# A gated linear recurrence and a squared-ReLU layer on one core: transfers of the first gates over three queues, the activation table loaded first, identity and mask made later, and a new order of the first 640 entries of the schedule

## The chip, the core and the metric

The kernel runs on one core of one Trainium2 chip. The core has five instruction queues that run side by side: TensorE (PE, matrix products; PEld is its weight load), VectorE (DVE), ScalarE (ACT), GpSimd (POOL) and SyncE (SP). Transfers between the device's memory and the core's on-chip memory are issued by SP, ACT or POOL and carried out by 16 DMA engines. The metric is the device time of one execution in microseconds (us); lower is better.

## The reference

Two blocks follow each other. The first keeps, for each of 4 x 8 heads, a complex 48 x 48 state that is multiplied at each of 768 steps by a complex gate (with its magnitude held below 0.999), takes in the product of key and value, and is read out by the query. The second is a two-layer network with a squared ReLU on the 3072 x 384 result.

```python
mag = np.sqrt(a_re * a_re + a_im * a_im)
scale = np.minimum(mag, 0.999) / (mag + 1e-06)
a_re_n, a_im_n = (a_re * scale, a_im * scale)
for t in range(S):
    new_re = ar * S_re - ai * S_im
    new_im = ar * S_im + ai * S_re
    kv = np.einsum('bhd,bhe->bhde', k[:, :, t], v[:, :, t])
    S_re, S_im = (new_re + kv, new_im)
    y[:, :, t] = np.einsum('bhd,bhde->bhe', q[:, :, t], S_re)
...
h = np.maximum(x @ w_in, 0.0)          # x: 3072 x 384, w_in: 384 x 2048
return (h * h @ w_out)                  # w_out: 2048 x 384
```

The inputs q, k, v, a_re and a_im are float32; the two weight matrices arrive as float64 and are turned into float32 on the chip.

## The kernel before

Each sequence of 768 tokens is cut into 6 chunks of 128 tokens. Two chunks of two sequences (b = 0 and b = 1) make a group, and there are 12 groups (gi = 0 to 11). A group goes through three stages. First its operands are made by DVE and ACT: the gates are normalised, their running products inside a chunk are built in blocks of eight steps, and queries and keys are multiplied with them. Then each chunk is worked by PE: products of keys and queries, a causal mask on DVE, products with the values, and the new state. Last, the two layers are applied to the group's 256 tokens: for each part of the hidden layer a product with w_in (lines 1052 and 1068), a squared ReLU on ACT, and products with w_out (line 1088 for the first two groups, line 1158 later, where seven half products with sums of halves stand in for eight).

Nothing here is ordered by a compiler. The string FRONT is a list of some 1,380 entries, written out by hand, and `follow` calls the function of each entry in turn. Every engine therefore works through its instructions in the order of the list, and waits on semaphores only for what another engine or a transfer has to deliver. An entry is a letter with numbers. Those that matter here:

- `l0.0.0` and `l0.0.1` load the gates (a_re and a_im) of group 0 for b = 0 and b = 1; `l0.1.0` and `i0.1.0` load its queries and keys, the upper heads by SP and the lower by POOL. Each load is one transfer of 48 rows ("whole") and two or more of 16 rows ("gap"), in lines 527 and 532.
- `f0` fetches the first block of weight words by SP and `j0` the rest of the same block by POOL in two transfers (line 695); `f2`, `j2` and so on do it for other blocks. Three blocks are held at a time.
- `p0.k` and `q0.k` are the steps of making group 0's operands for b = 0 and b = 1. On ACT: p0.0 squares (L776), p0.1 and p0.2 the parts in the blocks' order (L761), p0.4 inverse root (L795), p0.5 (L799), p0.8 and p0.9 (L761), p0.10 (L822), p0.12 negated imaginary parts (L836), p0.14 keys (L853, L761). On DVE: p0.3 (L790), p0.7 (L494, L808), p0.11 the gates (L828, L494, L832), p0.13 (L848), p0.15 the first step in blocks (L494), p0.17 and p0.19 totals and carries, p0.20 and p0.28 to p0.30 the products. p0.21 sends the last heads by SP (L904).
- `U0` and `S0` take the low and high part of weight block 0 on ACT (L621, L628); `D0` and `A0` decode it on DVE (L635 and a custom instruction). The parts are kept in two places, so U4 overwrites what A2 reads.
- `a0.0` to `a0.9` are the work on group 0's first chunk: a0.0 scores on PE (L948), a0.1 and a0.3 transposes on PE with the identity (L956), a0.5 the product with the mask on DVE, a0.6 values on PE (L975), a0.7 the copy of the tokens on ACT (L986), a0.8 what is added to the state (L999, with two small instructions on POOL, L1005). `b0.k` is the second chunk.
- `g0.0` moves rows of x to their places with two transfers by SP (L1044), after which `F0.1.0` is the first long product on PE (L1052) and `H0.1.0` its squared ReLU.
- `M0` to `M8` are small preparations. M0 is an activation whose only use is that its table is loaded; M1 turns the causal mask on ACT and PE (lines 572 to 577); M2 to M8 set tiles to zero on DVE.

Before the list starts, POOL makes the identity and a plain triangular mask (lines 547 to 556), and DVE sets a few constants.

Of the kernel before, what the change touches and what calls it, by code (L numbers as in the profile page):

```python
# [27 lines left out]
ALU = mybir.AluOpType  # L28
# [398 lines left out]
def quotient_path(ctx, tc, feat, vtok, w_in, w_out, w1, w2, out, n_seq, count):  # L427

    nc = tc.nc
# [75 lines left out]
    def load_parts(gi, part=None, second=False, only=None):  # L505
# [7 lines left out]
        for b, n in enumerate(groups[gi]):  # L513
            if only not in (None, b):
                continue
            for hh, queue in enumerate(queues):
                if queue is None:
                    continue
                gap = raw[pads(hh), parts, b]
                rest = feat[n, hh].rearrange("(r g) x p t -> r x g p t", g=NG)[:, parts, :, NG]  # L520
                pieces = [(slice(None), i) if gap.shape[1] < NG else (slice(None), slice(None), i)
                          for i in range(min(gap.shape[1:3]))]
                moves = [(gap[at], rest[at]) for at in pieces]
                whole = (raw[rows(hh), parts, b].rearrange("d x g t -> d x (g t)"),
                         feat[n, hh, :, parts, 0:NG].rearrange("d x g t -> d x (g t)"))
                if part == 0 and b:
                    queue.dma_start(out=whole[0], in_=whole[1])
                    queue = nc.gpsimd
                else:
                    moves.insert(len(moves) if part == 0 else 0, whole)  # L530
                for to, of in moves:
                    queue.dma_start(out=to, in_=of)

    def in_turn(rows_, n):

# [3 lines left out]
    def load_values(gi, only=None):  # L539
        for b, n in enumerate(groups[gi]):  # L540
            if only not in (None, b):
# [15 lines left out]

    def turn_mask(step):
        if step == 0:

            nc.scalar.activation(out=sums[:, 0:1], in_=tiny, func=AF.Abs_reciprocal_sqrt)
            return
        if step > 1:

# [579 lines left out]
    def half_product(i, z):  # L1144
        if z == 0:
            o_of[i, 0] = po.tile([P, DM], F32, tag="o", name="o_ps")
        if z == 1:
            o_of[i, 1] = ph.tile([P, 2, TOK], F32, tag="h", name="o_ps").rearrange(
                "p j t -> p (j t)")
        lower = range(KH // 2)  # L1150
# [11 lines left out]
    def outputs(i, r):  # L1162
# [2 lines left out]
                out_of[i, b] = ffn.tile([P, DM], F32, name="o")  # L1165
        o, left, right = [out_of[i, b] for b in range(GC)], slice(0, MH), slice(MH, DM)
        chain = o_of[i, 0][:, 0:MH]
        others = [o_of[i, 1][:, k * MH:(k + 1) * MH] for k in range(2)] if r else None
        if r == 0:
            twice(o[0][:, left], chain)  # L1170
        elif r == 1:
# [18 lines left out]


    FRONT = (
        "l0.0.0 l0.0.1 M1 M0 p0.0 p0.1 p0.3 p0.4 p0.5 p0.7 M2 M3 p0.2 q0.0 q0.3 M8 M6 M7 p0.9 "
        "p0.8 q0.4 p0.10 q0.5 p0.11 l0.1.0 f0 f1 f2 i0.1.0 j0 j2 q0.1 p0.12 q0.7 p0.15 D0 p0.23 "
        "p0.24 p0.25 U0 q0.10 p0.6 p0.22 q0.8 p0.13 S0 q0.9 q0.2 p0.14 p0.16 A0 U2 p0.26 M5 j1 "
        "i0.1.1 U1 S1 S2 D2 p0.27 q0.11 p0.17 j3 i1.2.0 j4 q0.12 p0.18 D1 q0.15 p0.19 l0.1.1 "
        "q0.22 f3 l1.2.0 v0.0 f5 q0.23 p0.28 q0.24 M4 p0.20 q0.25 p0.29 q0.16 p0.30 q0.26 q0.13 "
        "q0.27 p0.21 f4 a0.1 a0.0 A1 q0.17 a0.5 A2 q0.14 q0.6 p1.6 a0.2 U3 a0.3 a0.4 q0.18 S3 "
        "a0.6 l1.2.1 q0.19 U4 a0.7 S4 D3 D4 A3 i1.2.1 j5 j6 j7 a0.8 p1.0 q0.28 p1.3 q0.20 q1.0 "
        "D5 q0.29 q1.3 q0.30 U5 p1.4 p1.5 g0.0 f6 F0.1.0 S5 q0.21 p1.7 A4 a0.9 b0.1 p1.2 p1.10 "  # L1200
        "p1.8 p1.9 p1.1 U6 b0.2 p1.11 A5 b0.0 f7 v0.1 p1.12 H0.1.0 S6 U7 p1.22 p1.15 b0.5 p1.23 "
        "D6 p1.24 D7 f8 F0.0.0 b0.6 b0.3 b0.7 S7 b0.4 H0.0.0 p1.25 A6 p1.16 A7 F0.2.0 b0.8 U8 "
        "H0.2.0 S8 F0.3.0 p1.26 D8 p1.27 p1.13 p1.17 p1.14 H0.3.0 q1.4 p1.18 A8 f10 g0.1 v1 f9 "
        "f11 F0.3.1 F0.2.1 q1.5 H0.3.1 U9 U10 H0.2.1 S10 S9 p1.19 p1.28 p1.20 p1.29 D11 p1.30 "
        "q1.7 D10 D9 b0.9 T0.0.0 F0.0.1 F0.1.1 p1.21 f12 f13 v2 a1.1 q1.2 q1.8 q1.1 q1.9 a1.2 "
        "q1.10 A10 A9 U11 q1.11 a1.0 a1.5 a1.3 q1.12 U12 a1.4 S11 q1.15 q1.23 D12 q1.24 A11 "
        "q1.25 T0.1.0 a1.6 a1.7 S12 g1.0 f15 f14 q1.22 A12 q1.16 D13 q1.26 q1.27 q1.13 q1.17 "
        "a1.8 T0.2.0 T0.3.0 T0.4.0 U13 H0.0.1 q1.6 H0.1.1 q1.14 S13 F1.2.0 H1.2.0 F1.1.0 i2 "
        "q1.18 A13 q1.19 q1.28 q1.20 D14 q1.29 q1.30 U14 U15 H1.1.0 S14 S15 A14 l2 q1.21 D15 "
        "A15 F1.0.0 T0.5.0 F1.3.0 T0.6.0 T0.7.0 o2.0 o2.1 H1.0.0 a1.9 o2.3 E0.0 o2.4 o2.5 o2.7 "  # L1210
        "o2.2 b1.1 b1.0 b1.5 o2.8 o2.9 H1.3.0 b1.2 o2.10 o2.11 o2.12 o2.15 o2.23 o2.24 o2.25 "
        "T0.0.1 T0.1.1 T0.2.1 T0.3.1 T0.4.1 T0.5.1 T0.6.1 T0.7.1 b1.3 b1.6 o2.22 E0.1 b1.4 o2.6 "
        "b1.7 b1.8 o2.13 o2.14 o2.16 o2.26 o2.27 o2.17 o2.18 o2.19 o2.20 o2.28 o2.29 o2.30 g1.1 "
        "s0.0 l3 T1.0.0 T1.1.0 T1.2.0 T1.3.0 T1.4.0 T1.5.0 T1.6.0 T1.7.0 F1.0.1 H1.0.1 E1.0 "
        "F1.2.1 o3.0 o3.3 b1.9 w0 o2.21 T1.0.1 F1.1.1 T1.1.1 a2.3 o3.1 o3.4 o3.5 o3.2 H1.1.1 "
        "H1.2.1 a2.4 o3.7 t0 a2.0 F1.3.1 T1.2.1 a2.1 a2.5 o3.9 o3.8 a2.2 a2.6 a2.7 o3.10 a2.8 "
        "b2.0 t1 o3.11 T1.3.1 b2.5 b2.6 H1.3.1 W0 o3.22 T1.4.1 T1.5.1 T1.6.1 T1.7.1 o3.12 o3.13 "
        "a2.9 o3.15 b2.7 o3.6 o3.14 g2 F2.3 H2.3 F2.5 F2.7 H2.5 o3.23 o3.24 o3.25 o3.16 o3.26 "
        "o3.27 o3.17 o3.18 o3.19 o3.20 o3.28 o3.29 o3.30 H2.7 F2.6 b2.3 H2.6 b2.4 l4 s0.1 F2.0 "
        "b2.1 F2.4 H2.0 o4.0 H2.4 o4.3 X2.3 X2.0 F2.1 Z2.1 o4.4 o4.5 E1.1 H2.1 t3 o4.6 b2.2 "  # L1220
        "o4.2 o4.1 o3.21 s1.1 v3 w2 s1.0 a3.0 X2.1 o4.7 Y2.3 a3.5 Y2.0 Y2.1 F2.2 H2.2 o4.8 b2.8 "
        "a3.6 b2.9 Z2.0 a3.1 a3.7 R2.0 o4.9 o4.10 a3.2 X2.2 t2 Q2.0 Q2.3 Y2.2 Z2.3 b3.0 a3.3 "
        "o4.11 o4.12 o4.15 b3.5 Q2.1 a3.4 R2.3 Z2.2 b3.6 a3.8 o4.23 o4.24 Q2.2 a3.9 o4.22 R2.2 "
        "b3.7 o4.13 o4.14 Z2.4 Z2.5 g3 F3.4 o4.25 o4.16 R2.5 R2.1 R2.4 o4.26 o4.27 o4.17 l5 v4 "
        "H3.4 F3.7 o4.18 H3.7 F3.0 b3.3 W2 b3.4 H3.0 Z2.6 F3.3 H3.3 o4.19 X3.0 Y3.0 o4.20 o4.28 "
# [24 lines left out]
        "o8.20 o9.0 H7.4 F7.2 F7.6 H7.2 o8.29 X7.1 o8.30 o9.3 o9.4 o9.5 o9.7 Y7.1 o9.1 Z6.6 "  # L1250
# [150 lines left out]
```

## Time and profile before

| what | us |
|---|---|
| median of 3 runs (660.87 to 662.35) | 661.85 |
| the profiled execution, as timed | 661.44 |
| its span, from the first to the last instruction | 659.1 |
| PE busy in it | 611.2 |
| DVE busy | 492.1 |
| ACT busy | 434.2 |
| first squares of the gates on ACT begin | 7.36 |
| first product with the mask on DVE begins | 41.95 |
| first long product of the network on PE begins | 50.46 |

The span leaves out what lies ahead of the first and behind the last instruction. A line of the timeline gives start, length, engine, line of the code, operation, output and input; what stands in brackets is the idle time before it and what ended it. The chain of waits is followed backwards from the last instruction, from each piece of work to the one that released it. In the stretches, busy times of the five engines stand side by side.

### The profile page before, as it was taken

What the parts mean: (1) busy time and instruction counts of PE and PEld (TensorE: products, weight loads), DVE (VectorE), ACT (ScalarE), POOL (GpSimd) and SP (SyncE); (2) the same over time, 40 slices, a digit from 0 to 9 for tenths busy, and PEclk for the clock granted to TensorE, in tenths of its full rate; (3) what the DMA queues carried; (4) which work ended last, traced back from release to release, by engine and by line L of the source; (5) the groups of instructions that cost most, each with busy time, mean ns of one, the idle gap of its engine ahead of it and who ended that gap; (6) DMA issues with size and microseconds to landing.
All of it is one profiled execution on the core that took longest, in us unless ns stands there. A gap on an engine that the chain in (4) does not pass through costs nothing.

```text
span 659.1 us, 14644 instructions
## 1 busy us (share of the span) xinstructions
PE 611.2 (93%) x5915; PEld 549.0 (83%) x5915; DVE 492.1 (75%) x981; ACT 434.2 (66%) x847; POOL 33.2 (5%) x74
## 2 busy tenths in 40 slices
PE   0059999999999999999999999999999999999995
PEld 0048987687899899889899899899899899999995
DVE  4999997998999948968759858879859858743030
ACT  7669998568584676593686685686785575544330
POOL 5232120000000000000000000000000000000000
PEclk9999999999999999999999999999999999999999
DMA  8968682360640820631832813542731730233101
GB/s 192 192 132 218 188 226 41 59 103 24 92 98 10 154 62 7 121 74 30 137 129 56 153 40 94 93 111 78 108 87 32 109 75 12 67 85 84 44 25 30
DMA packets 41750, 60.50 MB, mean 92 GB/s; under 512 B 5832, under 2 KB 29896, under 8 KB 41672
## 3 DMA queue, kind: packets, MB, share of 16 engines
q1 hardware_dynamic: 39496, 55.49, 39.2%
q0 software_dynamic: 1824, 3.64, 2.9%
q8 instruction: 48, 0.79, 0.5%
q10 hardware_dynamic: 352, 0.34, 0.2%
q14 instruction: 30, 0.25, 0.1%
HBM read 48.76 MB, written 4.72 MB: 81 GB/s over the span
## 4 chain that ended last, share of the span: by engine, by line
PE 77%; DVE 10%; ACT 6%; DMA 5%; issue 1%; SPq 0%; DVEq 0%; ACTq 0%
PE h_ps L1068 29%; PE o_ps L1158 27%; PE a_ps L948 5%; PE h_ps L1052 4%; PE y L975 3%; DMA raw<-in_feat_dram 3%; PE y L939 3%; DVE ab L494 2%; PE add L999 2%; DVE pr L494 2%; PE tp L956 2%; PE o_ps L1088 1%; DMA words<-in_moe_w_out_dram 1%; ACT room L761 1%; ACT ab L761 1%; DVE room L494 1%
## 5 line engine op out<-in xcount | busy, mean ns | idle before, releaser
L1068 PE MATMUL h_ps<-x,w 128*128 128x256 f32 x960 | 213.1, 380 | 0.1
L1068 PEld LDWEIGHTS h_ps<-x,w 128*128 128x128 f32 x960 | 180.6, 190 | 25.3 <-ACT h L1075 1.1
L1158 PE MATMUL o_ps<-w,h 128*128 128x192 f32 x640 | 110.5, 328 | 0.2 <-ACT o L1031 0.2
L1158 PEld LDWEIGHTS o_ps<-w,h 128*128 128x128 f32 x640 | 103.7, 190 | 2.5 <-issue 1.4
L1075 ACT ACTIVATE h<-h_ps 128x512 f32<-128x512 f32 x80 | 47.6, 595 | 57.8 <-PE h_ps L1068 56.7
L494 DVE TENSOR_TENSOR pr<-ab 128x384 f32<-128x384 f32 (+3 forms) x196 | 70.1, 375 | 3.4
L1158 PE MATMUL o_ps<-w_sum,mix 128*128 128x192 f32 x320 | 55.2, 327 | 0.0
L494 DVE TENSOR_TENSOR ab<-pr 128x48 f32<-128x48 f32 (+3 forms) x210 | 49.9, 260 | 5.3
L1076 ACT ACTIVATE h<-h 128x512 f32<-128x512 f32 x80 | 50.6, 632 | 2.6
L1158 PEld LDWEIGHTS o_ps<-w_sum,mix 128*128 128x128 f32 x320 | 51.8, 190 | 0.6 <-issue 0.3
L1052 PEld LDWEIGHTS h_ps<-x,w 128*128 128x128 f32 x384 | 46.4, 200 | 5.4 <-ACT room L776 3.7
L1052 PE MATMUL h_ps<-x,w 128*128 128x128 f32 x384 | 47.2, 285 | 3.6 <-DMA x<-x 3.6
L494 DVE TENSOR_TENSOR a<-a_ps,mask 128x1024 f32<-128x1024 f32 x24 | 29.3, 1221 | 27.6 <-PE a_ps L948 27.4
L956 PE MATMUL tp<-ident,qk 128*128 128x128 f32 x120 | 21.1, 286 | 30.8 <-DVE qk L494 30.7
L494 DVE TENSOR_TENSOR qk<-ab,qk 128x768 f32<-128x768 f32 (+1 forms) x56 | 46.2, 841 | 1.0
L956 PEld LDWEIGHTS tp<-ident,qk 128*128 128x128 f32 x120 | 15.0, 145 | 35.9 <-issue 32.7
L1088 PE MATMUL o_ps<-w,h 128*128 128x384 f32 x128 | 43.8, 490 | 0.0
L761 ACT ACTIVATE qk<-raw 128x768 f32<-128x768 f32 (+1 forms) x28 | 36.9, 1343 | 5.2 <-DVE raw L494 5.2
L761 ACT ACTIVATE room<-z 128x768 f32<-128x768 f32 (+1 forms) x28 | 36.8, 1373 | 5.1 <-DVE z L808 5.1
L494 DVE TENSOR_TENSOR mix<-h 128x256 f32<-128x256 f32 x40 | 16.8, 421 | 31.0 <-ACT h L1076 30.8
L494 DVE TENSOR_TENSOR room<-ab,carry 128x1344 f32<-128x1344 f32 (+1 forms) x28 | 36.8, 1354 | 3.0 <-ACT carry L877 2.5
L761 ACT ACTIVATE ab<-raw 128x768 f32<-128x768 f32 (+1 forms) x28 | 37.8, 1375 | 0.5 <-DVE qk L494 0.3
(105 smaller groups left out, 912.4 us busy)
## 6 DMA issues: line engine op xcount, KB each, us to landing
raw<-in_feat_dram SPq DMA_DIRECT2D x40, 288.0 KB
words<-in_moe_w_out_dram SPq DMA_DIRECT2D x8, 768.0 KB
again<-in_moe_w_in_dram SPq DMA_DIRECT2D x16, 384.0 KB
again<-in_moe_w_out_dram SPq DMA_DIRECT2D x16, 384.0 KB
last<-qk SPq DMA_DIRECT2D x48, 97.5 KB
words<-in_moe_w_in_dram SPq DMA_DIRECT2D x8, 576.0 KB
vt<-in_vtok_dram SPq DMA_DIRECT2D x24, 192.0 KB
out_dram<-o SPq DMA_DIRECT2D x23, 192.0 KB
```

Of the source, the lines that this page charges most:

```text
L494: nc.vector.tensor_tensor(out=out, in0=in0, in1=in1, op=op)
L761: nc.scalar.activation(out=out.rearrange("p c j n -> p c n j"), func=AF.Copy, in_=in_.rearrange("p c (n j) -> p c n j", j=L), **kwargs)
L939: nc.tensor.matmul(ys[p_ % 2][crossed(hh, p_), p_ // 2], lhsT=states[b][1 - c_seq % 2][rows(hh), c, columns(hh, p_ * ROWS + PAD)], rhs=ope ...
L948: nc.tensor.matmul(ps[s, hh, p_], lhsT=operand(2 + c, p_, rows(hh))[:, s], rhs=operand(c, p_, rows(hh)), start=(c == RE), stop=(c == IM), ...
L956: nc.tensor.transpose(tp[:, g], qk_of[gi % 2][:, b, g, 2 + c, 0:C], ident)
L975: nc.tensor.matmul(tiles["y"][p_ % 2][crossed(hh, p_), p_ // 2], lhsT=v[:, columns(hh, at)], rhs=tiles["am"][:, hh, p_], start=(first and ...
L1052: nc.tensor.matmul(ps[:, j], lhsT=w1_blocks[:, k, g, at:at + P], rhs=x_of[i][:, g, b * C:(b + 1) * C], start=(g == 0), stop=(g == NG - 1))
L1068: nc.tensor.matmul(ps[:, j], lhsT=w1_blocks[:, k, g, at:at + P], rhs=x_of[i][:, g], start=(g == 0), stop=(g == NG - 1))
L1075: nc.scalar.activation(out=h, in_=h_ps[i, f], func=AF.Relu, scale=of_w1)
L1076: nc.scalar.activation(out=h, in_=h, func=AF.Square)
L1088: nc.tensor.matmul(o_of[i, b], lhsT=tokens_of(i, f, b)[:, j], rhs=w2[:, k], start=(k == 0), stop=(k == NFB - 1))
L1158: nc.tensor.matmul(to, lhsT=x(k)[:, j], rhs=factor(z)[:, 2 * k + j], start=(z in (0, 1, 3) and k == j == 0), stop=(k == KH // 2 - 1 and j ...
```

## The change

Five things are edited.

1. For the gates of b = 0, the first of each half's two gap transfers is issued by POOL; the six transfers are two each on SP, ACT and POOL.
2. Identity and plain mask are no longer made ahead of the list, but by a new entry M9.
3. In the list, M0 comes ahead of the gates' second load, and M9 and M1 come some 80 entries later.
4. The first 637 entries of the list have a new order. The rest, 742 entries, is as before.
5. The tile for the second half of the outputs is taken by whichever of the half products 1, 3 and 5 comes first, and an output step looks at that tile only if it uses it, so that these may be in another order.

```diff
-                for to, of in moves:
-                    queue.dma_start(out=to, in_=of)
+                for i, (to, of) in enumerate(moves):
+                    (nc.gpsimd if part == 0 and b == i == 0 else queue).dma_start(out=to, in_=of)
...
-    make_identity(nc, ident)
...
-    nc.gpsimd.memset(plain, 1.0)
-    nc.gpsimd.affine_select(out=plain, in_=plain, pattern=[[-1, C]], compare_op=ALU.is_ge, fill=0.0,
-                            base=0, channel_multiplier=1)
...
+        if step == 9:
+            make_identity(nc, ident)
+            nc.gpsimd.memset(plain, 1.0)
+            nc.gpsimd.affine_select(out=plain, in_=plain, pattern=[[-1, C]], compare_op=ALU.is_ge,
+                                    fill=0.0, base=0, channel_multiplier=1)
+            return
...
-        if z == 1:
+        if z in (1, 3, 5) and (i, 1) not in o_of:
...
-    others = [o_of[i, 1][:, k * MH:(k + 1) * MH] for k in range(2)] if r else None
+    others = [o_of[i, 1][:, k * MH:(k + 1) * MH] for k in range(2)] if r % 2 else None
...
-        "l0.0.0 l0.0.1 M1 M0 p0.0 p0.1 p0.3 p0.4 p0.5 p0.7 M2 M3 p0.2 q0.0 q0.3 M8 M6 M7 p0.9 "
-        "p0.8 q0.4 p0.10 q0.5 p0.11 l0.1.0 f0 f1 f2 i0.1.0 j0 j2 q0.1 p0.12 q0.7 p0.15 D0 p0.23 "
-        "p0.24 p0.25 U0 q0.10 p0.6 p0.22 q0.8 p0.13 S0 q0.9 q0.2 p0.14 p0.16 A0 U2 p0.26 M5 j1 "
-        "i0.1.1 U1 S1 S2 D2 p0.27 q0.11 p0.17 j3 i1.2.0 j4 q0.12 p0.18 D1 q0.15 p0.19 l0.1.1 "
-        "q0.22 f3 l1.2.0 v0.0 f5 q0.23 p0.28 q0.24 M4 p0.20 q0.25 p0.29 q0.16 p0.30 q0.26 q0.13 "
-        "q0.27 p0.21 f4 a0.1 a0.0 A1 q0.17 a0.5 A2 q0.14 q0.6 p1.6 a0.2 U3 a0.3 a0.4 q0.18 S3 "
-        "a0.6 l1.2.1 q0.19 U4 a0.7 S4 D3 D4 A3 i1.2.1 j5 j6 j7 a0.8 p1.0 q0.28 p1.3 q0.20 q1.0 "
...
+        "M8 l0.0.0 M7 M0 l0.0.1 p0.0 p0.1 p0.3 M2 p0.4 p0.5 p0.7 p0.2 q0.0 j2 j0 i0.1.0 l0.1.0 "
+        "f0 f2 q0.3 p0.8 p0.9 p0.10 q0.4 q0.5 p0.11 q0.7 j1 U0 p0.12 q0.10 q0.8 S0 p0.22 q0.9 "
+        "q0.1 p0.6 q0.2 M4 p0.15 D0 p0.23 M3 p0.24 M6 p0.25 D2 p0.16 M5 A0 p0.26 p0.13 p0.27 "
+        "q0.11 p0.17 l0.1.1 f1 p0.14 U1 q0.12 U2 S1 p0.18 i0.1.1 S2 q0.6 q0.22 i1.2.0 M9 j4 j3 "
+        "M1 D1 p0.19 q0.15 p0.28 q0.23 p0.20 q0.24 A1 q0.25 p0.29 q0.16 p0.30 q0.26 q0.13 q0.27 "
+        "A2 q0.17 l1.2.0 v0.0 f4 f3 p0.21 f5 a0.1 a0.0 p1.6 a0.2 q0.14 U4 S4 U3 a0.3 a0.5 a0.6 "
+        "q0.18 S3 a0.4 a0.7 D3 q0.19 A3 a0.8 p1.0 q0.20 p1.3 q0.28 j5 i1.2.1 j6 D5 q0.29 D4 "
...
```

Further on in the list, entries that the text below names stand so: before, `... p1.25 A6 p1.16 A7 F0.2.0 b0.8 U8 H0.2.0 S8 F0.3.0 ...` (shortened); after, `F0.2.0` is followed by `F0.3.0`, `F0.2.1` and `F0.3.1`, and `b0.8` comes behind them.

## The prediction

> **What bounds the kernel now.** I read the page's busy times and slices first, then the table of stretches, the chain of waits, the timeline of the first 20 us, and the landings of the earliest transfers.
>
> ```profile
> span 659.1 us, 14644 instructions
> PE 611.2 (93%) x5915; PEld 549.0 (83%) x5915; DVE 492.1 (75%) x981; ACT 434.2 (66%) x847; POOL 33.2 (5%) x74
> PE   0059999999999999999999999999999999999995
> ```
>
> TensorE is busy 611.2 of 659.1 us. The stretches show where the other 47.9 us lie (columns: length, then busy time and count of PE, PEld, DVE, ACT, POOL; clock; DMA share; GB/s).
>
> ```profile
> 0.00:8.20 8.20, 0.47 (x1) 0.18 (x1) 0.58 (x5) 4.29 (x7) 7.12 (x20) 1.00 0.66 155
> 8.20:13.20 5.00, 0.00 (x0) 0.00 (x0) 3.60 (x16) 4.97 (x10) 2.38 (x5) 1.00 1.07 246
> 13.20:42.00 28.80, 5.46 (x70) 4.36 (x70) 27.49 (x97) 18.35 (x38) 6.22 (x12) 1.00 0.87 171
> 42.00:50.40 8.40, 3.66 (x48) 3.50 (x48) 8.37 (x14) 7.37 (x16) 3.95 (x8) 1.00 0.85 143
> 60.00:75.00 15.00, 15.00 (x158) 14.27 (x157) 14.27 (x41) 14.36 (x33) 0.00 (x0) 1.00 0.63 203
> ```
>
> Before 50.4 us TensorE is idle 40.8 us; from there to 640 us it is full in nearly every stretch, and the last 6.7 us are outside the changed entries. Fifteen of 15 us busy could hide waiting, so I checked 163.82 to 174.2: 48 products of L1068 take 10.36 us on the chain, 216 ns each, as everywhere later. The order after 50.4 can therefore win next to nothing; it can only lose. What can be won is the start of the first long product, F0.1.0:
>
> ```profile
> 2.47 3.36 DMA raw<-in_feat_dram
> 13.31 0.45 DVE room L828
> 42.03 1.13 DVE a L494
> 45.15 0.21 ACT x L986
> 46.49 3.73 DMA x<-x
> 50.46 5.26 PE h_ps L1052 x24
> ```
>
> From 13.2 us to the mask product a0.5 (begins 41.95) VectorE works 27.5 of 28.8 us: that stage is its length. What is ahead of 13.2 is ScalarE's:
>
> ```profile
> 0.80 2.26 SPq L532 DMA_DIRECT2D raw<-in_feat_dram  x3
> 3.30 1.28 ACT L572 ACT_TABLE_LOAD   x1 [3.30 <-issue]
> 4.60 0.40 ACT L572 COPY mask<-plain 128x128 f32<-128x128 f32 x1
> 5.56 0.37 ACT L576 COPY mask<-turned 128x128 f32<-128x128 f32 x1 [0.56 <-PE turned L575]
> 5.95 1.28 ACT L561 ACT_TABLE_LOAD   x1
> 7.36 0.83 ACT L776 ACTIVATE room<-raw 128x768 f32<-128x768 f32 x1
> 14.78 0.48 ACT L836 ACTIVATE ab<-ab 128x336 f32<-128x336 f32 x1
> 15.17 1.05 ACT L621 ACTIVATE part<-words 128x768 int16<-128x768 uint32 x1
> ```
>
> The gates landed at 5.83 (2.47 + 3.36); ScalarE took them at 7.36, after two table loads and the mask.
>
> **The change, step by step.** *Six transfers, three queues.* The whole rows go out second on SP instead of third: the second issue starts at 1.60, and with the same 3.36 us they land at 4.96. POOL's two gap rows start at 0.80 (identity and mask no longer ahead); its first such row took 2.7 us, so they are in by 4.5. ScalarE issues two (to 2.2), loads one table (1.28), does the tiny activation (0.20) and issues one more (0.44): free at 4.1. The squares start at 5.0 for 7.36, 2.36 us sooner.
>
> *Table and mask.* One load (1.28) and the two mask copies with the transpose between (5.05 to 5.93) leave the front. They return as M9 (four POOL instructions, 0.99 us) and M1. POOL idles 12.7 us and 7.8 us between 12 and 40 us; ScalarE waits 7.4 us in one piece for DVE (ends L853, to 37.5). M1, 1.3 us, lies in that piece; without it the price is 1.3 us on the way to the mask product. M9 stands ahead of j4 and j3 on POOL, which wait for buffers anyway.
>
> *Memsets.* M7 and M8 (0.39 each) go into DVE's 6.7 us of waiting, M2 (0.70) into its wait of 1.2 us before p0.7. p0.7 then ends at 11.16 - 2.36 = 8.80; q0.0 runs 8.2 to 9.0, p0.8 and p0.9 take 1.51 and end near 10.4: p0.11 starts at 10.5 for 13.23. That is 2.7 us won at this point. M3 and M6 (0.28) go into the packed stretch, and A2 (0.88 on the chain) moves ahead of a0.5. Unhindered, a0.5 starts at 10.5 + 28.72 (41.95 - 13.23) + 0.28 + 0.88 = 40.4, 1.55 us sooner.
>
> *The wait that takes its place.* On ScalarE the new list has U0 (L621, first weight words) ahead of p0.12 (L836); before, it came after. p0.15 on DVE needs p0.12, and all of DVE stands behind p0.15. If words0 lands at time L, p0.12 ends at L + 1.05 + 0.48; DVE would be ready at 10.5 + (16.19 - 13.23) = 13.5. So each us of L beyond 12.0 costs one. Words0 comes in one part by SP and two by POOL, and the new list puts j2 before j0 on POOL.
>
> ```profile
> words<-in_moe_w_in_dram POOLq DMA_DIRECT2D x1, 96.0 KB, 6.2
> words<-in_moe_w_in_dram POOLq DMA_DIRECT2D x2, 96.0 KB, 8.6
> ```
>
> Issued from 5.48 on, the four parts land at 11.7, 14.3, 15.3 and 16.5 in the trace (the lines are for the first, and the second and third together). Words0's last part was POOL's ninth transfer, 14.3; it becomes the tenth. The late bound: the tenth landed at 15.3, POOL starts 0.87 us sooner (0.80 for 1.67), 14.4. The early bound: the first seven landed 4.3 to 9.8, 0.9 us apart; going on so, the tenth comes at 4.3 - 0.87 + 9 x 0.9 = 11.6, if POOL gets through before the 576 KB of f0 fill the engines. I take the middle, L = 13.0: p0.12 ends at 14.5, DVE stands 1.0 us, a0.5 starts at 41.4: 0.55 us of the 2.7 are left. At 11.6 it is 1.55, at 14.4 a loss of 0.8.
>
> *From a0.5 to F0.1.0.* U4 and S4 move ahead of U3 on ScalarE, before a0.7. U4 overwrites the part that A2 reads, so it now starts after the earlier A2. Counted from the end of q0.13: A2 ends 1.5 us later, then U4, S4, U3 (1.05 each), q0.18 (0.7), S3 (1.06), a0.4 (0.7): a0.7 at 7.1; TensorE's way (a0.5 3.95 us later, then 3.06 as before) gives 7.0. Loss 0.1. The gap transfer took 3.73 us behind two loads of the next chunk; POOL's half of these is now issued after a0.8's work there, which waits for p0.21's landing, some 2 us later than now. Bounds: nothing, and 1.0 (last<-qk landed in 2.8). I take 0.3. F0.1.0 comes 0.55 - 0.1 + 0.3 = 0.75 us sooner.
>
> *After it.* F0.3.0 loses b0.8 (1.09) in front of it; A7, which it needs, ended 1.08 before it. DVE is 0.55 + 0.88 = 1.4 ahead there, TensorE 0.75 + 1.09 = 1.84: 0.65 us of slack stay. F0.1.0's own 24 products take 5.26 us, those at 57.96 only 2.88; it starts behind the same kind of idle stretch as before, so I leave that as it is. The new order of half products and outputs change order, not counts. I put nothing for them, bounds 0 and 1 us lost.
>
> *Sum.* The profiled execution took 661.44; less 0.75 it is 660.7. The median is 0.41 above that execution, so 661.1.
>
> The Trainium skill (DMA: Bandwidth & Descriptors, Issuing engines are not separate DMA queues) holds that queues share the same 16 engines and spreading saves issue time alone. The trace has those engines full from 8.2 to 13.2 (share 1.07). By that rule words0 would land no sooner than now, 14.3, and the sum would be 0.6 us over before, 662.4.
>
> The skill (ScalarE: Activation LUTs, What ACT_TABLE_LOAD costs) counts 1.38 us of drain with each load; here the copy starts 0.02 us after the load, and the row decides. By the page the squares would start at 5.5, which the stall on U0 would swallow: the same sum.
>
> **Rivals.** *Words in time* (0.36): L below 12.5, and at 12.0 DVE doesn't stand at all; with the gap transfer 0.3 to 1.0 sooner it is then 1.55 - 0.1 + 0.3 (or 1.0), 1.75 to 2.45 won, 660.1 to 659.4. For it: POOL starts 0.87 sooner and the small rows come first. Against: the engines are full from 3.5 us on.
>
> *Words late* (0.24), the other side: L is 15.6, the eleventh's landing less 0.87, because each POOL part waits for a long stretch of f0 and f2. ScalarE stands in U0 until then, with p0.12, q0.10, q0.8, S0 behind it and DVE behind p0.12: p0.12 ends at 17.1, DVE stands 3.6 us, a0.5 comes at 44.0, F0.1.0 2.05 + 0.1 - 0.3 = 1.85 later: 663.7. It decides from L = 15.1 (then 1.3 us are lost).
>
> *The start doesn't reach TensorE* (within the forecast): the 2.36 us all go into U0's wait and the gap transfer lands as before: 661.9. The forecast with this neighbour, L from 12.5 to 15.0, holds 0.40, from 660.6 to 663.1.
>
> **How the numbers follow.** 0.2% of 661.85 is 1.3 us, about what a measurement of this kernel can tell. Forecast 661.1 (0.40, no change that can be told), faster 0.36, slower 0.24. The range goes from the early rival's end, 659.4, to the late one's 663.7.
>
> **What would show it.** Right: squares near 5.0; p0.11 near 10.5; L836 on ScalarE after L621, and DVE idle about 1 us ahead of the first L494 after L808; M1 in ScalarE's wait near 30 us; a0.5 near 41.4; h_ps L1052 first near 49.7; then the same count of busy TensorE. Wrong: no DVE gap there (the first rival) or one over 3 us (the second); a wait of TensorE over 0.5 us after the first h_ps, above all at F0.3.0, or the first x<-x landing later than 4.5 us after its issue.

## The result and the profile after

Before: 661.04 us, the median of 18 runs (659.83 to 662.97). After: 662.89 us, the median of 18 runs (661.99 to 664.75). The ratio is 1.0025, 95% interval 1.0017 to 1.0034: the change made the kernel slower, by 1.85 us by the medians and by some 1.7 us by the ratio.

The profiled execution of after took 664.75 us, the slowest of its 18 runs, so the differences in it are about 1.5 us larger than typical; the profiles of the experiments show where that lies. First the header and the busy times of its page, and the same stretches as were shown of before (length, then busy time and count of PE, PEld, DVE, ACT, POOL; clock; DMA share; GB/s):

```profile
span 662.5 us, 14643 instructions
PE 611.8 (92%) x5915; PEld 549.2 (83%) x5915; DVE 491.7 (74%) x981; ACT 434.1 (66%) x846; POOL 33.2 (5%) x76
```

```profile
0.00:8.20 8.20, 0.00 (x0) 0.00 (x0) 2.56 (x15) 3.83 (x6) 5.99 (x15) 1.00 0.72 147
8.20:13.20 5.00, 0.00 (x0) 0.00 (x0) 3.21 (x6) 4.58 (x10) 2.61 (x5) 1.00 1.06 221
13.20:42.00 28.80, 3.69 (x50) 3.10 (x52) 24.75 (x82) 17.32 (x35) 6.27 (x14) 1.00 0.84 154
42.00:50.40 8.40, 6.31 (x75) 4.80 (x71) 8.12 (x24) 7.60 (x16) 4.67 (x10) 1.00 1.09 199
60.00:75.00 15.00, 15.00 (x183) 14.54 (x176) 12.90 (x39) 14.73 (x30) 0.00 (x0) 1.00 0.57 195
```

TensorE's busy time is the same within 0.6 us (611.2 before), and it is full from 60 us on (589.55 of the 590 us from 60 to 650). The loss is ahead of that, and the third stretch shows it: VectorE works 24.75 of 28.8 us where it worked 27.49. The timelines of ScalarE and VectorE show the hole (start, length, engine, line, operation; in brackets the idle time and what ended it):

```profile
2.17 1.28 ACT L557 ACT_TABLE_LOAD   x1 [2.17 <-issue]
3.46 0.20 ACT L557 ACTIVATE sums<-tiny 128x1 f32<-128x1 f32 x1
5.82 0.84 ACT L778 ACTIVATE room<-raw 128x768 f32<-128x768 f32 x1 [2.16 <-DMA raw<-in_feat_dram]
...
16.40 1.06 ACT L623 ACTIVATE part<-words 128x768 int16<-128x768 uint32 x1 [3.43 <-DMA words<-in_moe_w_in_dram]
17.34 0.45 ACT L838 ACTIVATE ab<-ab 128x336 f32<-128x336 f32 x1
```

```profile
11.63 0.56 DVE L830 SCALAR_TENSOR_TENSOR room<-room 128x384 f32<-128x384 f32 x1 [0.84 <-ACT room L763]
...
17.82 0.36 DVE L494 TENSOR_TENSOR pr<-ab 128x192 f32<-128x192 f32 x1 [3.08 <-ACT ab L838]
```

U0 (L623 now, L621 before) stands 3.43 us for words0, p0.12 (L838) stands behind it, and VectorE stands 3.08 us for p0.12. The chain of waits of after goes the same way: from POOL's issues to the landing of the words, and further on through the gap transfer of x:

```profile
4.59 1.50 POOL words L697 x3
6.09 10.24 DMA words<-in_moe_w_in_dram
16.40 1.06 ACT part L623
...
44.54 1.23 DVE a L494
...
48.95 4.85 DMA x<-x
53.94 5.34 PE h_ps L1054 x24
```

In the trace f0, SP's part of words0, landed at 13.30; POOL's four parts, j2's two ahead of j0's two, landed at 10.39, 12.21, 15.46 and 16.33. Set beside before, in us from the span's start:

| start of | before | after | difference |
|---|---|---|---|
| squares of the gates, p0.0 | 7.36 | 5.82 | -1.54 |
| p0.11 | 13.23 | 11.63 | -1.60 |
| p0.15 (first L494 after the wait) | 16.19 | 17.82 | +1.63 |
| product with the mask, a0.5 | 41.95 | 44.54 | +2.59 |
| first copy of the tokens, a0.7 | 45.01 | 47.41 | +2.40 |
| first long product, F0.1.0 | 50.46 | 53.94 | +3.48 |
| F5.0, first group behind the changed entries | 316.50 | 320.53 | +4.03 |
| last half product, Z11.6 | 649.65 | 653.45 | +3.80 |

So 1.6 us were won at the front, 3.2 lost at U0, 1.0 lost up to a0.5, 0.9 between a0.5 and F0.1.0 (0.2 won up to a0.7, 1.1 lost behind it), and 0.3 behind F0.1.0 by the end. Three theories stand from here: U0's wait is the loss; A2 and U4, moved ahead, are; or the transfers of later data are, which make x<-x land late (4.85 us after its issue for 3.73).

### The profile page after: what moved, and what is told of

Same layout as the page of the kernel before. It is cut to its first block, busy times and chain, and to the rows that moved or that the text cites. A ratio compares the mean times of both kernels' runs of the same rounds, so it can differ in the third digit from the quotient of the medians.

```text
span 662.5 us, 14643 instructions
## 1 busy us (share of the span) xinstructions
PE 611.8 (92%) x5915; PEld 549.2 (83%) x5915; DVE 491.7 (74%) x981; ACT 434.1 (66%) x846; POOL 33.2 (5%) x76
## 4 chain that ended last, share of the span: by engine, by line
PE 84%; DMA 6%; DVE 4%; ACT 3%; issue 1%; POOL 1%; SPq 1%; DVEq 0%; ACTq 0%; POOLq 0%
PE h_ps L1070 29%; PE o_ps L1160 27%; PE a_ps L950 6%; PE h_ps L1054 6%; PE o_ps L1090 6%; PE y L977 4%; PE y L941 3%; DMA words<-in_moe_w_in_dram 3%; PE add L1001 3%; PE tp L958 2%; DMA raw<-in_feat_dram 1%; DMA words<-in_moe_w_out_dram 1%; DVE ab L494 1%; DVE pr L494 1%; DMA x<-x 1%
## 5 line engine op out<-in xcount | busy, mean ns | idle before, releaser
L494 DVE TENSOR_TENSOR pr<-ab 128x384 f32<-128x384 f32 (+3 forms) x196 | 70.1, 375 | 9.3 <-ACT ab L838 6.3
L494 DVE TENSOR_TENSOR ab<-pr 128x48 f32<-128x48 f32 (+3 forms) x210 | 50.0, 260 | 5.3
L494 DVE TENSOR_TENSOR a<-a_ps,mask 128x1024 f32<-128x1024 f32 x24 | 29.3, 1221 | 29.7 <-PE a_ps L950 29.6
L494 DVE TENSOR_TENSOR qk<-ab,qk 128x768 f32<-128x768 f32 (+1 forms) x56 | 46.3, 841 | 1.0
L494 DVE TENSOR_TENSOR room<-ab,carry 128x1344 f32<-128x1344 f32 (+1 forms) x28 | 36.7, 1353 | 3.3 <-ACT carry L879 2.9
L988 ACT COPY x<-y 64x256 f32<-64x256 f32 (+1 forms) x72 | 26.5, 368 | 19.3 <-PE y L977 17.9
L494 DVE TENSOR_TENSOR mix<-h 128x256 f32<-128x256 f32 x40 | 16.8, 419 | 29.2 <-ACT h L1078 29.2
L950 PE MATMUL a_ps<-qk 48*64 48x128 f32 x1152 | 38.3, 275 | 0.0
```

The lines of the kernel that those rows point to most:

```text
L494: nc.vector.tensor_tensor(out=out, in0=in0, in1=in1, op=op)
L950: nc.tensor.matmul(ps[s, hh, p_], lhsT=operand(2 + c, p_, rows(hh))[:, s], rhs=operand(c, p_, rows(hh)), start=(c == RE), stop=(c == IM), ...
L988: nc.scalar.copy(out=x_of[gi][to, odd::2, b * C:(b + 1) * C], in_=tiles["y"][odd][of, 0:NP // 2])
```

## The experiments

Every kernel was timed in five rounds against before on the same chip. The diffs give the list's edits only; "..." leaves out what is unchanged. In the tables L is the landing of the last part of words0, and p0.15, a0.5 and F0.1.0 are starts, all from the one profiled execution.

**First set: one thing put right in the kernel after, or the front alone.**

e1_j0_first

```diff
-... q0.0 j2 j0 i0.1.0 ...
+... q0.0 j0 j2 i0.1.0 ...
```

> The kernel after, with one swap: POOL issues j0, the parts of words0, ahead of j2. Theory 1 (U0's wait on ScalarE is the loss): in the profile of after the places that j0 then takes landed at 10.4 and 12.2 and f0 at 13.3, so words0 is complete at about 13.3 instead of 16.3. U0 ends near 14.4, p0.12 near 14.8, VectorE stands about 0.1 us ahead of p0.15 instead of 3.1, and what follows comes 3.0 sooner; D2 may then wait some 0.7 us for words2. That is about 2.3 us less than after, so 0.5 us less than before: ratio to before 0.999. Theory 2 (what is lost is lost later, in the transfers that land late ahead of F0.1.0 and in A2 and U4 ahead of a0.7): VectorE's 3 us disappear, but the first x<-x still lands near 53 us; ratio 1.002 as after.

e2_U0_later

```diff
-... U0 p0.12 q0.10 q0.8 S0 p0.22 ... p0.15 D0 p0.23 M3 p0.24 M6 p0.25 D2 ...
+... p0.12 q0.10 q0.8 p0.22 U0 S0 ... p0.15 p0.23 M3 p0.24 M6 p0.25 D0 D2 ...
```

> The kernel after, with U0 and S0 behind p0.12, q0.10, q0.8 and p0.22 on ScalarE, and D0 behind p0.25 on VectorE; no transfer is moved. Theory 1: words0 still lands near 16.3, but p0.12 ends near 13.5 and p0.15 starts when VectorE is done with q0.7, at 14.7 instead of 17.8; D2 may wait 0.7 us for words2, so F0.1.0 comes 2.3 to 3 us sooner than after: ratio to before 0.998 to 0.999. Theory 2 (the loss lies in the later transfers, in A2 or in U4): ratio 1.002 as after, with p0.15 at 14.7 all the same.

e3_front_alone (the list of before, edited; the code of after)

```diff
-l0.0.0 l0.0.1 M1 M0 p0.0 p0.1 p0.3 ... q0.3 M8 M6 M7 p0.9 ... i0.1.1 U1 ... q0.22 f3 ...
+M8 l0.0.0 M7 M0 l0.0.1 p0.0 p0.1 p0.3 M2 ... q0.3 M6 p0.9 ... i0.1.1 M9 U1 ... q0.22 M1 f3 ...
```

> The list of before, with only the front of the change: the six transfers over three queues, M0 ahead of the gates' second load, M8, M7 and M2 in VectorE's early waits, M9 behind i0.1.1 on POOL and M1 behind q0.22 on ScalarE. Theory 1 (the front won 1.6 us at p0.11 and the new order lost it): p0.11 near 11.6, p0.15 near 14.7 (16.2 before), a0.5 and F0.1.0 about 1.5 us sooner than before: ratio 0.9977. Theory 2 (the front's gain can't reach the first product, since the transfers of later data fill the 16 engines and the last<-qk and x<-x transfers land when they did): x<-x lands near 50 as before and the ratio is 1.000. Theory 3 (M1 and M9 cost where they now stand): 1.3 us on ScalarE or POOL ahead of a0.5, ratio 1.000 to 1.002.

e4_loads_first

```diff
-... A3 a0.8 p1.0 q0.20 p1.3 q0.28 j5 i1.2.1 j6 D5 ...
+... A3 j5 i1.2.1 j6 a0.8 p1.0 q0.20 p1.3 q0.28 D5 ...
```

> The kernel after, with j5, i1.2.1 and j6 ahead of a0.8 in the list, so that POOL issues these eight transfers without waiting first for the last heads' transfer (10.8 us of waiting in the profile of after). Theory 1 (U0's wait is the loss, the rest small): the transfers of the first x<-x land in 3.7 us instead of 4.9, which gives back at most 1.1 us; VectorE still stands about 3 us ahead of p0.15: ratio to before 1.001 to 1.0025. Theory 2 (the late loads ahead of x<-x are the loss): ratio 1.000 or below.

| kernel | ratio to before, interval | L | p0.15 | a0.5 | second x<-x, start of issue to landing | F0.1.0 |
|---|---|---|---|---|---|---|
| after | 1.0025, 1.0017 to 1.0034 | 16.33 | 17.82 | 44.54 | 4.9 | 53.94 |
| e1_j0_first | 1.0011, 0.9999 to 1.0023 | 12.54 | 15.15 | 41.83 | 3.9 | 50.30 |
| e2_U0_later | 1.0014, 1.0001 to 1.0027 | 15.41 | 14.82 | 41.63 | 5.1 | 51.32 |
| e3_front_alone | 0.9999, 0.9988 to 1.001 | 16.04 | 14.82 | 41.90 | 3.6 | 50.18 |
| e4_loads_first | 1.0026, 1.0013 to 1.0039 | 15.54 | 17.02 | 44.98 | 2.5 | 52.07 |

Two edits that have nothing in common but that U0 no longer holds p0.12 up give back about the same: 1.2 and 1.3 of the 1.85 us by the medians, each against its own runs of before, and 0.9 and 0.7 us by the ratios, whose intervals overlap that of after. (A clearer price of this wait is e14's, in the fourth set.) In e1 the swap brings words0 in 3.8 us sooner, and U0 starts as soon as ScalarE is free, with no wait in brackets:

```profile
13.37 1.05 ACT L623 ACTIVATE part<-words 128x768 int16<-128x768 uint32 x1
14.29 0.46 ACT L838 ACTIVATE ab<-ab 128x336 f32<-128x336 f32 x1
```

Theory 1 had expected both to get below before, and neither does: something else costs about as much as the front won.

e3 missed as well. The front alone is worth nothing in the list of before: p0.15 is 1.4 us sooner, but D0 on VectorE and U0 on ScalarE then stand until words0 is in, at 16.04, and a0.5 is where it was.

```profile
16.12 0.56 DVE L637 TENSOR_SCALAR w<-words 128x768 int32<-128x768 int32 x1 [0.66 <-DMA words<-in_moe_w_in_dram]
13.58 0.48 ACT L838 ACTIVATE ab<-ab 128x336 f32<-128x336 f32 x1
16.11 1.08 ACT L623 ACTIVATE part<-words 128x768 int16<-128x768 uint32 x1 [2.05 <-issue]
```

e4 shows the other resource: x<-x lands in 2.5 us, but last<-qk, now behind the same loads, lands 5.0 us after its issue began (2.8 before), and a0.5 waits for it. The wait moved from one small transfer to another, and the time is that of after. As for L, the kernels that keep after's order of these transfers have 15.41 (e2), 15.54 (e4) and, below, 14.89 (e6) and 14.99 (e14); 16.33 in the profile of after is the late end, 0.9 us above the middle of the five, and so probably a part of why its execution is the slowest.

**Second set: A2 put back, and the front's way cleared in the list of before.**

e5_j0_A2 is e1 with the second diff below; e6_A2_back is after with that diff alone.

```diff
-... q0.27 A2 q0.17 ... q0.14 U4 S4 U3 a0.3 a0.5 a0.6 q0.18 S3 a0.4 a0.7 D3 ...
+... q0.27 q0.17 ... q0.14 U3 a0.3 a0.5 A2 a0.6 q0.18 S3 a0.4 U4 a0.7 S4 D3 ...
```

> The kernel after with two edits: j0 ahead of j2 on POOL, and A2 back behind a0.5 with U4 and S4 around a0.7 as before. Theory 1 (three terms add up: words0 landing late, about 0.9 us against before at p0.15; A2 ahead of a0.5, 0.95; U4 and S4 ahead of a0.7, 0.24): from the run with j0 ahead of j2 (a0.5 41.83, a0.7 45.13) a0.5 comes to about 40.9, a0.7 to 44.0, F0.1.0 to about 49.2; time about 1 us under that run: ratio to before 0.9995. Theory 2 (A2 and U4 were hidden behind the transfers that x<-x waits for): a0.5 comes sooner but x<-x lands near 50 all the same, ratio 1.001 as in that run.

> The kernel after with A2 back behind a0.5 and U4 and S4 around a0.7 as before; the transfers stay as they are. Theory 1: p0.15 still near 17 to 17.8, since words0 lands as in after (15.5 to 16.3); a0.5 and a0.7 about 1 us sooner than after: about 0.9 to 1.2 us less than after, ratio 1.001. Theory 2 (U0's wait alone is the loss, the rest is hidden): ratio 1.0025 as after.

e7_front_U0 and e8_front_j0, each one edit of e3_front_alone:

```diff
-... p0.15 D0 p0.23 p0.24 p0.25 U0 q0.10 p0.6 p0.22 q0.8 p0.13 S0 ...
+... p0.15 p0.23 p0.24 p0.25 q0.10 p0.6 p0.22 q0.8 D0 U0 p0.13 S0 ...
```

```diff
-... l0.1.0 f0 f1 f2 i0.1.0 j0 j2 ...
+... l0.1.0 f0 f1 f2 j0 i0.1.0 j2 ...
```

> The list of before with the front of the change, as in the run of the front alone, and D0, U0 and S0 later: behind p0.25 on VectorE and behind q0.8 on ScalarE. Theory 1 (the front's 1.4 us were lost because words0 lands at 16.1 and D0 and U0 stand waiting for it): no wait for words0, p0.23 at 15.4 and p0.13 near 17.5 instead of 19.1; a0.5 near 40.7, F0.1.0 1.2 us sooner than in the run of the front alone: ratio 0.998. Theory 2 (later transfers set F0.1.0 whatever VectorE does): a0.5 near 40.7, x<-x near 50, ratio 1.000.

> The list of before with the front of the change, and j0 ahead of i0.1.0 on POOL; D0 and U0 stand where they stood. Theory 1 (the landing of words0 decides): j0's two parts go in the places that landed at 10.2 and 12.5 in the run with j0 ahead of j2, so words0 is in at about 12.6; D0 at 15.4 and U0 near 14.1 without a wait; a0.5 near 40.6, ratio 0.998, as with D0 and U0 later. Theory 2 (later transfers decide): words0 near 12.6, ratio 1.000. Theory 3 (i0.1.0 is now late: its three transfers land 1 to 2 us later and q0.1 or p0.22 waits): a wait on ScalarE of 1 us or more for raw, ratio 1.000.

| kernel | ratio to before, interval | L | p0.15 | a0.5 | second x<-x, start of issue to landing | F0.1.0 |
|---|---|---|---|---|---|---|
| e5_j0_A2 | 1.0009, 0.9995 to 1.0023 | 12.16 | 14.64 | 40.80 | 6.0 | 51.43 |
| e6_A2_back | 1.0039, 1.0026 to 1.0053 | 14.89 | 16.38 | 42.52 | 5.1 | 52.25 |
| e7_front_U0 | 0.9987, 0.9975 to 1.0 | 15.88 | 14.65 | 40.59 | 3.5 | 48.79 |
| e8_front_j0 | 0.9981, 0.997 to 0.9992 | 12.22 | 14.67 | 40.77 | 4.0 | 49.47 |

e7 and e8 settle the first point: with the wait for words0 out of the way, by either edit, the front's gain arrives at a0.5 (1.2 to 1.4 us sooner than before), at F0.1.0 (1.0 to 1.7 us), and in the time: e8 is 1.5 us faster than before, e7 1.1 us, with an interval that just reaches 1. That both do excludes M1 and M9, which stand in e7 and e8 where e3 has them, as the cause of e3's miss. U0 of e8 follows p0.12 without a gap:

```profile
13.43 0.48 ACT L838 ACTIVATE ab<-ab 128x336 f32<-128x336 f32 x1
13.81 1.04 ACT L623 ACTIVATE part<-words 128x768 int16<-128x768 uint32 x1
```

e5 went by theory 2. e6 fits neither theory: theory 1 expected 1.001 and theory 2 1.0025, and it came out at 1.0039, though its profile has a0.5 and F0.1.0 sooner than the profile of after. Its interval overlaps that of after, and no run shows a cause. In e5 A2 back brings a0.5 1.0 us sooner than in e1 (41.83 to 40.80), but x<-x, issued 0.9 us sooner, takes 2.0 us longer and lands later.

```profile
45.35 5.95 DMA x<-x
51.43 4.71 PE h_ps L1054 x24
```

**Third set: the order of the later transfers, the order behind F0.1.0, and the queues.** The order of after leaves the DMA engines idle for three microseconds and fills them later (after, columns as above, DMA share second to last):

```profile
23.00:26.00 3.00, 0.00 (x0) 0.00 (x0) 2.90 (x8) 1.52 (x4) 0.00 (x0) 1.00 0.01 3
26.00:30.00 4.00, 0.00 (x0) 0.00 (x0) 3.65 (x17) 3.13 (x4) 3.46 (x9) 1.00 0.78 157
30.00:34.00 4.00, 0.27 (x1) 0.18 (x1) 3.93 (x9) 3.39 (x11) 1.78 (x4) 1.00 1.10 173
```

f4, f3, j4 and j3 are issued at 28.6 to 31.7 there, behind l1.2.0 and i1.2.0, which can't be issued before 25.9, when ScalarE has read the rows that they overwrite (p0.14); f4's own buffer is free earlier (e9 issues f4 at 17.0). And i1.2.1, j5 and j6 are issued up to 5 us ahead of x<-x. e9_loads is e5 with:

```diff
-... q0.22 i1.2.0 M9 j4 j3 ... l1.2.0 v0.0 f4 f3 ... a0.8 p1.0 q0.20 p1.3 q0.28 j5 i1.2.1 j6 ... j7 g0.0 ...
+... q0.22 f4 j4 i1.2.0 M9 j3 ... l1.2.0 v0.0 f3 ... j5 i1.2.1 a0.8 p1.0 q0.20 p1.3 q0.28 ... g0.0 j6 j7 ...
```

> The kernel with j0 ahead of j2 and A2 back (the first run of the second set), with the order of later transfers changed as well: f4 and j4 ahead of i1.2.0 and l1.2.0, j5 and i1.2.1 ahead of a0.8, j6 and j7 behind g0.0. Theory 1 (in the new order x<-x lands late because j6 and i1.2.1 are issued within 3 us ahead of it and the engines are full until 51): f4 is issued near 18 instead of 25.4, x<-x lands about 3.5 us after its issue instead of 5.8, F0.1.0 starts near 49.2 instead of 51.4: about 2 us less, ratio to before 0.998. Theory 2 (the same bytes must pass before x<-x whatever their order): x<-x lands near 51 as there, ratio 1.001.

e10_new_tail is e8 up to F0.1.0 and has all later entries in the order of after. e12_new_head_old_tail is e9 up to F0.1.0 and has the later entries in the order of before; q1.3, q0.30 and f6, which before has ahead of F0.1.0, come right behind it.

> The list of before with the front of the change and j0 ahead of i0.1.0, up to F0.1.0; all entries behind F0.1.0 in the order of after. Theory 1 (behind F0.1.0 the new order loses 0.6 us: from b0.1 to F5.0 261.4 to 261.7 us in the five profiles with the new order, 260.8 to 261.1 in the four with the old): F5.0 0.6 us later than in the run with the old order behind F0.1.0; ratio to before 0.999 instead of 0.998. Theory 2 (the order behind F0.1.0 is worth nothing, the difference comes from the state at F0.1.0): 0.998 as there.

> The head of the run with the later transfers in another order (new order with j0 ahead of j2, A2 back, f4 and j4 early, j6 and j7 behind g0.0), and behind F0.1.0 the order of before. Theory 1 (head and tail add): F0.1.0 as in that run, near 49.2, and 0.6 us less behind it: ratio 0.997 to 0.998. Theory 2 (head and tail don't add, because the entries that the head leaves over come due early in the old tail): a wait of TensorE over 0.5 us behind F0.1.0, ratio 1.000 or above.

e11_two_queues is e8 with one line of the change undone:

```diff
-                    (nc.gpsimd if part == 0 and b == i == 0 else queue).dma_start(out=to, in_=of)
+                    queue.dma_start(out=to, in_=of)
```

> The list of before with the front of the change and j0 ahead of i0.1.0, with one edit of the change undone: the first gates' gap transfers go by SP and ACT again, none by POOL. Theory 1 (the engines, not the queues, set when the gates land): SP's whole rows third again, landing near 5.8; the squares start 0.1 to 0.4 us later than with three queues (5.7), p0.11 as much later, and the ratio to before stays 0.998 to 0.999. Theory 2 (the third queue is what won the front): squares near 7, p0.11 near 13, ratio 1.000.

| kernel | ratio to before, interval | L | p0.15 | a0.5 | second x<-x, start of issue to landing | F0.1.0 |
|---|---|---|---|---|---|---|
| e9_loads | 0.9983, 0.9972 to 0.9994 | 12.10 | 14.76 | 40.75 | 3.0 | 48.39 |
| e10_new_tail | 0.9992, 0.998 to 1.0004 | 12.47 | 14.88 | 40.70 | 3.6 | 49.00 |
| e11_two_queues | 0.9991, 0.9977 to 1.0005 | 14.84 | 15.45 | 41.44 | 3.9 | 50.09 |
| e12_new_head_old_tail | 1.0, 0.9985 to 1.0015 | 12.57 | 14.76 | 42.31 | 2.6 | 49.59 |

e9 hit: 0.9983 from 1.0009, with VectorE's work in the same places. The chain and one stretch (43 to 46 and 46 to 48 us) of e9:

```profile
45.30 2.96 DMA x<-x
48.39 4.54 PE h_ps L1054 x24
```

```profile
43.00:46.00 3.00, 2.46 (x42) 2.33 (x38) 2.97 (x5) 2.93 (x7) 1.08 (x2) 1.00 0.94 169
46.00:48.00 2.00, 0.00 (x0) 0.00 (x0) 2.00 (x5) 2.00 (x5) 0.00 (x0) 1.00 0.21 52
```

and the same stretch of e5:

```profile
43.00:46.00 3.00, 2.43 (x42) 2.31 (x40) 2.97 (x5) 2.93 (x6) 1.55 (x4) 1.00 1.05 158
46.00:48.00 2.00, 0.00 (x0) 0.00 (x0) 2.00 (x4) 2.00 (x4) 0.00 (x0) 1.00 1.08 139
```

TensorE, VectorE and ScalarE do the same in both; between 46 and 48 the DMA share is 0.21 in e9, where x<-x lands in 3.0 us, and 1.08 in e5, where it goes beside words and rows that nobody needs yet and takes 6.0. One part of e9's edit moved nothing: POOL issues j6 at 43.88 in e9 and at 43.98 in e5, ahead of x<-x in both. What moved are f4 (17.0 for 25.4), j4 (17.3 for 26.5), j5 (29.2 for 40.3) and i1.2.1 (38.8 for 41.4); which of these it takes is not shown.

e10: with the new order behind F0.1.0 the time is 0.7 us above e8's by the ratios, and b0.1 to F5.0 takes 261.35 us for 260.76. The two intervals overlap, but the profiles agree: from b0.1 to F5.0 the ten kernels with the new order there have 261.15 to 262.53, of the six with the old order five have 260.62 to 261.14 and one (e12) 261.38. No single wait of TensorE behind the first x<-x is over 0.3 us in after, so these 0.6 us are not pinned to a place.

e11 fell between: without POOL's share the squares start at 6.81 for e8's 5.66, 1.15 us later and not 0.1 to 0.4 as theory 1 had it; f0, behind more rows on SP, then sets L at 14.84, and F0.1.0 comes 0.6 us later. In the time e11 and e8 can't be told apart, since their intervals overlap. Only a part of the 1.15 us is issue time: the last transfer of these gates is issued at 2.47 for 2.06, 0.41 us later, but it lands after 4.24 us for 3.53, beside the rows of the other sequence, which POOL then issues from 1.38 on instead of 2.59. How the rest divides is not shown.

e12 went by theory 2: head and tail did not add, and TensorE waits 0.84 us behind F0.1.0, ahead of b0.1. The entry q1.3, which the new head leaves over and which stands first in e12's tail, makes VectorE wait 0.86 us for ScalarE's squares there, and the work that b0.1 needs stands behind it:

```profile
51.85 0.56 DVE L792 SCALAR_TENSOR_TENSOR room<-room 128x384 f32<-128x384 f32 x1 [0.86 <-ACT room L778]
55.88 0.52 PE L958 MATMUL tp<-ident,qk 128*128 128x128 f32 x3 [0.84 <-DVE pr L494]
```

From F0.1.0 to F5.0 the profile of e12, in an execution 1.2 us above its median, has 267.68 us for e9's 265.53. Another part of the difference comes ahead of F0.1.0. The head is e9's entry for entry, and still f3 landed at 39.44 for 37.20, last<-qk at 40.75 for 38.91, and a0.5 started at 42.31 for 40.75. So the landings of these full stretches vary by about 2 us between executions with the same code ahead of them; one profile of either can't separate 1 us there.

**Fourth set: single prices where x<-x is not late.** e14_j2_first is e9 with j2 ahead of j0 again; e13_A2_ahead is e9 with A2, U4 and S4 where after has them.

> The version with three things put right in the new order (j0 ahead of j2, A2 and U4 back, later transfers in another order), with one of them taken back: j2 ahead of j0 as in after. Theory 1 (U0's wait reaches F0.1.0 in full once x<-x is not late): words0 in at 15.4 to 16.3, p0.15 at 16.9 to 17.8 instead of 14.8, F0.1.0 2.1 to 3 us later; ratio to before 1.001 to 1.003 instead of 0.998. Theory 2 (part of the wait is slack): F0.1.0 at most 1 us later, ratio 0.999 to 1.000.

> The same version with another of the three taken back: A2 ahead of a0.5, and U4 and S4 ahead of U3, as in after. Theory 1 (A2 costs its length on the way to F0.1.0 when x<-x is not late): a0.5 near 41.7 instead of 40.75, F0.1.0 about 1 us later, ratio to before 0.9995 to 1.000 instead of 0.998. Theory 2 (A2 is hidden): a0.5 later but x<-x lands where it did, ratio 0.998.

| kernel | ratio to before, interval | L | p0.15 | a0.5 | second x<-x, start of issue to landing | F0.1.0 |
|---|---|---|---|---|---|---|
| e14_j2_first | 1.0003, 0.999 to 1.0017 | 14.99 | 16.49 | 42.44 | 2.8 | 49.90 |
| e13_A2_ahead | 0.9988, 0.9976 to 1.0 | 12.62 | 15.07 | 41.75 | 2.3 | 48.55 |

```profile
15.07 1.06 ACT L623 ACTIVATE part<-words 128x768 int16<-128x768 uint32 x1 [2.15 <-DMA words<-in_moe_w_in_dram]
```

The line is e14's: U0's wait is back, and F0.1.0 comes 1.5 us later, all of the 1.7 that p0.15 lost but 0.2; by the ratios it costs 0.20% (1.3 us). A2 ahead costs a0.5 its 1.0 us, F0.1.0 0.16, and the ratio stays within e9's interval: nothing that can be told. Three prices, then, each as one thing taken back from e9 at 0.9983: words0 late, to 1.0003 (0.20%); A2 and U4, to 0.9988 (0.05%); the later transfers, to 1.0009 (e5, 0.26%). By an estimate from the intervals each of them is good to some 0.17%, so the first and the third stand clear of noise, the first only just. They sum to 1.0034, against 1.0025 measured for the kernel that has all three; the sum is good to some 0.3%, so it agrees, but it is no sharp test.

## Why the prediction went wrong

Forecast was 661.1, no change that can be told; it was 662.89, slower. The forecast counted from 661.85, the median of three runs of before, where eighteen gave 661.04; each counted from its own median, 0.75 us were to be won and 1.85 were lost. The time lies in the range, near the case called words late (663.7), which had 0.24 and also has 1.85 us lost. That case had the right wait, U0's for words0 with L = 15.6, but that the numbers are equal is luck: it has the gap transfer 0.3 us sooner, which came 1.1 later. The steps, one by one:

- *Squares near 5.0.* Measured 5.82 (5.66 to 6.12 in the experiments with the three queues, e11 apart). POOL did not start at 0.80 but at 1.38, and the gates' last rows landed at 5.75. The order of the steps held; p0.11 came 1.6 us sooner, not 2.7. Since p0.15 waits for words0, this changes nothing at p0.15.
- *L = 13.0, between 11.6 and 14.4.* **This is the step that failed.** Measured 14.9 to 16.3 in the five profiles with after's order of these transfers (after, e2, e4, e6, e14; middle 15.4). Both bounds counted POOL's transfers, large and small alike: the late one by the tenth landing of before, the early one by the 0.9 us between the first seven, of which six are rows of 24 KB. But j0's last part went from second to fourth of POOL's words; the four land 0.9 to 3.3 us apart in after, and in before the fourth landed at 16.50. POOL's head start was 0.29 us, not 0.87, and it brought little: the fourth part of the words was issued at 6.09 for 7.04, 0.95 us sooner, and landed at 16.33 for 16.50, 0.17 sooner. What j0's place is worth is shown by the swap: 12.1 to 12.6 with j0 first (e1, e5, e9, e12, e13).
- *Each us of L beyond 12.0 costs one.* The slope is right: p0.12 and p0.15 follow U0 as worked out, p0.15 1.48 to 1.50 us behind L in after, e4, e6 and e14. The point from which it costs was not 12.0 but 13.2, since VectorE is ready at 14.74 in after, not at 13.5. With L = 15.4 VectorE stands 2.2 us, with the profile's 16.33 it stands 3.08, for the 1.0 of the forecast.
- *A2 ahead of a0.5 costs 0.88, U4 0.1.* A2's size at a0.5 is right (1.0 in e1 against e5 and in e13 against e9). U4 costs nothing there: from a0.5 to the first copy of a0.7 it is 2.87 us in e13 with U4 ahead and 3.06 in e9 without. (The 0.24 that the expectation of e5 gives U4 and S4 came from setting the second copy of e1, at 45.13, beside the first of before; e1's first is at 44.69.) On the way to the first product both together are worth nothing that can be told (e13).
- *The gap transfer 0.3 sooner, bounds nothing and 1.0.* Wrong in sign: 4.85 us in after for 3.73, 5.95 in e5, 2.96 in e9 where only the transfers' order differs. It was costed from POOL's issues being later alone. What was missed, as a second step that failed, is that f4, j4, f3 and j3 go behind l1.2.0 and i1.2.0 (28.6 for the first of these fetches, where before issued f3 at 20.0), and that j5 and i1.2.1, issued at 43.7 to 46.4, come within the 5.3 us ahead of x<-x, so that the backlog is still there. e5 to e9 prices such an order at 0.26%. That j6 too is issued ahead of x<-x in after, and behind it in before, does not make it late by itself, as e9 has it so.
- *The start can be hidden.* The neighbour inside the forecast, that the front doesn't reach TensorE, is what the front alone does in the list of before (e3, 0.9999).
- *M1, M9 and the memsets hidden.* Right: M1 at 33.3 in ScalarE's wait, M9 at 28.3 on POOL, M8 and M7 at 1.5, and VectorE has no wait on them. But j4 did not wait for its buffer there, as the prediction says it would: e9 issues it at 17.3, and in after it comes at 29.66, behind i1.2.0 and M9. What M9's 1.3 us on POOL cost by themselves is not shown.
- *Nothing behind F0.1.0, at most 1 us lost.* It is about 0.6 us lost by the profiles (e10 against e8), inside the bound.

The Trainium skill (DMA: Bandwidth & Descriptors, Issuing engines are not separate DMA queues) says that all queues share the same 16 engines and that spreading over queues saves issue time alone. The prediction worked out 662.4 by it and did not follow it; 662.89 was measured. That this is near is partly luck: the rule was taken to leave words0 at 14.3, and it landed at 14.9 to 16.3, since j2 went ahead of j0. The runs agree with the rule where the engines are full (0.95 us sooner in issue, 0.17 in landing). At the very front the third queue brought 1.15 us (e11), of which 0.41 is the sooner issue of the last of the six transfers.

## What to carry to other kernels

When an instruction is put ahead of another on its engine, what matters is the landing of what it waits for, and in a stretch where the transfer engines are full that landing is set by the large transfers ahead of it and hardly by its own issue: take the row of the transfer that stands in the same place among the large ones. A gain at the front arrives only if the next thing in the line has come too: here j0's two transfers, put ahead of the three of i0.1.0, turned a front worth nothing (0.9999) into 0.9981. And a small transfer that TensorE waits for is best issued ahead of its big neighbours: where j5, i1.2.1 and j6 were all issued in the six microseconds ahead of it (after, e1, e2, e5, e6), x<-x took 3.9 to 6.0 us, in the other eleven profiles 2.3 to 4.0.

## What the runs showed of the hardware

- In all sixteen profiles POOL has never more than eight of its transfers under way, and where nothing else holds it up, the next one is issued 0.28 us after the landing of the one eight places ahead: in after the eleventh at 7.58, the third having landed at 7.29; in before the twelfth at 7.95, the fourth having landed at 7.67. In e3 this put j0's second part, the eleventh there, at 7.96 and its landing at 16.04. The landings of POOL's transfers are told by eight semaphores in turn; whether the limit is the program's or the chip's is not shown.
- The 24 KB gap transfer took 2.3 to 6.0 us from issue to landing in these kernels, by what stood ahead of it.
- With the same entries ahead, f3 landed at 37.20 in one execution and at 39.44 in another (e9, e12), and words0 between 14.89 and 16.33 (after, e2, e4, e6, e14).
- F0.1.0's 24 products take 4.3 to 5.5 us in these profiles and 2.8 to 2.9 when they come again later. In the trace they follow each other every 213 ns or every 112, with few steps between, and the spread is how many of them go at which pace: in after all go at 213; in e3, e9, e8 and e1 the pace changes to 112 after 2.9, 3.5, 4.0 and 4.4 us; in e4, e7 and e13 the first four to eleven go at 112 and later ones at 213. The clock column doesn't follow this: it has 1.00 over F0.1.0 in before and 0.51 in after, at 213 ns in both. No rule for when the pace changes was found: the idle time of TensorE ahead of F0.1.0 was 3.6 us with 5.26 (before) and 3.6 us with 4.30 (e3).
